# A seventh place for side work behind each gate and up group, and another layout of the second layer's staging tiles

## The chip, the cores and the metric

The kernel runs on one core of a Trainium2 chip. Its engines work side by side, each through its own queue, in order: TensorE (PE, with its weight loads shown as PEld), VectorE (DVE), ScalarE (ACT), GpSimd (POOL) and SyncE (SP), which here only issues DMAs. The metric is the device time of one execution in microseconds (us), the median of several. All arithmetic is in fp32; a product is made of three matmuls on operands that are split into a rounded part and the rest.

## The reference

2048 tokens of width 1024. What is computed, with the shapes:

```python
xn  = layernorm(x)                          # [2048, 1024]
q, k, v = split(xn @ wqkv)                  # 32 heads of 32
pq, pk  = phi(q), phi(k)                    # phi(t) = where(t > 0, t + 1, exp(t)) + 1e-6
kv, z   = pk.T @ v, sum(pk)                 # for each head, over all tokens
s   = ((pq @ kv) / (pq @ z + 1e-6)) @ wo    # [2048, 1024]
h   = silu(xn @ w1) * (xn @ w3)             # [2048, 3584]
g   = silu(h @ w2)                          # [2048, 1024]
out = x + s * g
```

Both branches start from the same normalised `xn`, so the kernel normalises once.

## The kernel before, in words

**Products.** Every large product is done as one level of a Strassen-Winograd scheme: seven products of blocks (named B11, T2, T3, T1, B21, T4, B22 after the right operand, with A11, S2, S3, S1, A12, A22, S4 on the left) stand for eight, and sums of blocks are formed before and after. `split` (L84) makes an operand: a cast on ACT (L90), then the rest by a subtraction on DVE (L91). `mm3` (L95) issues the three matmuls, L98 to L100, of 128x128 by 128x512 each.

**First layer.** The tokens are taken in two halves of 1024 (`half`, L524). For each half, `gemm` (L400) is run for 4 pairs of keys and values, then for 4 query groups, then for 14 pairs of a gate and an up group; each group is 84 matmuls. Between its products a group calls `catch_up` (L388), which takes one piece of side work: first a kv step of the keys and values that lie behind (`later`), then one step of a generator of jobs (`jobs`), up to its next `yield`. The instructions of that step are put behind given marks on their engines with `tc.issue_after`. A group has six such places. In half 0 the jobs are `next_work` (L666): preparing the other half's operands and the sums of blocks of w2 (stored to `wt_d`). In half 1 they are `attention_work` (L817): z, the denominators, the product of kv with wo (`merge_wo`, stored to `wp_d`) and `divide` (L740), which loads a block of phi(q) and of the reciprocals into a tile, multiplies on DVE (L757), forms four sums (L603 to L607) and stores to `qs_d` on POOL (L760). `go_on` (L697) loads two jobs ahead. What is left at the end of a half is issued in one go (`for j, _ in jobs: run(j)`).

The job tiles (`job_tile`, L120) are three buffers. The signed tiles (`signed`, L117) are four buffers that hold phi and silu results; the small tiles (`small`, L114) are six, under the tag `c`.

**Attention layer and second layer.** Both use `Segment` (L849): the right operand is kept split, and eight groups of 256 tokens run past it (`tokens`, L881). The attention layer multiplies the stored query blocks by the stored kv-wo blocks (`wp`); its operands for the first token group are loaded into job tiles (`queries`, L972), and its output goes to `s_d` from small tiles. Another 32 steps of divides run in its own places. Then the first layer's pools are closed and the late pools are laid over them, in the order of their creation. The second layer, h @ w2, runs as five segments over 4, 6, 6, 6 and 6 blocks of 128 rows of w2. The right operand's pieces are loaded one at a time into staging tiles (`second_weights`, L992, load at L994) and split into `pw`; in the last token group of a segment the next segment's pieces are loaded and split (`between`, L1034). Left operands are loaded by `hiddens` (L985, load at L989) into twelve tiles. In the last segment `finish` (L1011) loads a block of s (`ss`, L1014) and, for the last token group, of x (`xs`, L1017), applies silu on ACT (L1018), multiplies on DVE (L1019) and stores, for all but the last token group by an accumulating DMA onto an `out` that was filled with x before (`lay_x`, L1026).

**Order.** The program is unrolled. The framework orders each engine's instructions, and each DMA queue's, ahead of time by its own simulated clock; on the chip each queue then goes strictly in that order, and an instruction that waits holds what stands behind it. `tc.issue_after(x)` adds an edge on the queue of x alone: later instructions of that engine are issued behind x, without waiting for its end. A late tile waits for the earlier tiles that lay on its bytes.

Of the kernel before, what the change touches and what calls it, by code (L numbers as in the profile page):

```python
# [9 lines left out]
F32 = mybir.dt.float32  # L10
# [6 lines left out]
P = 128  # L17
C = 512
# [4 lines left out]
def tile_linear_attention_times_swiglu(  # L23
# [10 lines left out]
    nc = tc.nc  # L34
    x, out = x[0], out[0]
# [15 lines left out]
    def bank(name):  # L51
        return ps.tile([P, C], F32, tag="bank", name=name)
# [27 lines left out]
    s_d = [dram.tile([P, D], F32, name=f"s_d{t}") for t in range(S // P)]  # L80
# [33 lines left out]
    def small(name):  # L114
        return pc.tile([P, C], F32, tag="c", name=name)
# [263 lines left out]
    def product(acc, B, A, start, stop=True):  # L379
        K = ND // 2  # L380
        for k in range(K):
            mm3(acc, (B[:, 0, k], B[:, 1, k]), (A[:, 0, k], A[:, 1, k]),
                start=start and k == 0, stop=stop and k == K - 1)
# [4 lines left out]
    def catch_up(*marks):  # L388

        if later:  # L390
            later.pop(0)()
        elif jobs:
            job, in_order = jobs[0]
            with ExitStack() as behind:
                for m in marks + (tuple(fetched) if in_order else ()):
                    behind.enter_context(tc.issue_after(m.ins))
                if next(job, None) is None:
                    jobs.pop(0)

    def gemm(B, A, use, early=False, paired=False, own=False):  # L400

        name = B.name
        B.upto("B11")
        u = (st.tile([P, C], F32, tag="own", bufs=1, name=f"u{name}") if own else  # L410
             pe.tile([P, C], F32, tag="u", name=f"u{name}"))
        ba = bank(f"a{name}")
        product(ba, B.upto("B11"), A["A11"], True)
        copied = nc.scalar.copy(out=u, in_=ba)
        if early:
            catch_up(copied)
            yield
            product(ba, B.upto("B21"), A["A12"], False)
            use(0, 0, ba)
            yield  # L420
            for _ in B.stages:
                pass
        else:
            next(stages, None)
            catch_up(copied)
            if paired:
                yield
        bb, bc, bd = (bank(f"{n}{name}") for n in "bcd")
        product(bb, B.upto("T2"), A["S2"], True)
        added = nc.vector.tensor_add(out=u, in0=bb, in1=u)  # L430
        next(stages, None)
        catch_up(copied, added)
        if paired:
            yield
        product(bc, B.upto("T3"), A["S3"], True)
        c22 = small(f"c22{name}")
        added = nc.vector.tensor_add(out=c22, in0=bc, in1=u)
        next(stages, None)
        catch_up(copied, added)
        if paired:  # L440
            yield
        product(bd, B.upto("T1"), A["S1"], True)
        added = nc.vector.tensor_add(out=c22, in0=bd, in1=c22)
        use(1, 1, c22)
        next(stages, None)
        catch_up(copied, added)
        if paired:
            yield
        if not early:
            product(ba, B.upto("B21"), A["A12"], False)  # L450
            use(0, 0, ba)
            next(stages, None)
            catch_up(copied, added)
        if paired:
            yield
        product(bc, B.upto("T4"), A["A22"], False)
        c21 = small(f"c21{name}")
        added = nc.vector.tensor_add(out=c21, in0=bc, in1=u)
        use(0, 1, c21)
        next(stages, None)  # L460
        catch_up(copied, added)
        if paired:
            yield
        product(bd, B.upto("B22"), A["S4"], False)
        c12 = small(f"c12{name}")
        nc.vector.tensor_add(out=c12, in0=bd, in1=u)
        use(1, 0, c12)
        next(stages, None)

    def phi(src, dst, z=None):  # L470

        nc.scalar.activation(dst, src, AF.Relu, scale=-1.0)
        nc.scalar.activation(dst, dst, AF.Exp, scale=-1.0)
        nc.vector.scalar_tensor_tensor(dst, src, 0.0, dst, op0=ALU.max, op1=ALU.add, accum_out=z)  # L474
# [49 lines left out]
    def half(h):  # L524
        A = operand_tiles(h)

        def keys(pair, **how):
            return gemm(ops[f"k{h}_{pair}_"], A, uses[pair][0], **how)

        def values(pair, **how):  # L530
            return gemm(ops[f"v{h}_{pair}_"], A, uses[pair][1], **how)
# [44 lines left out]
        for pair in range(ND // 2):  # L576

            def use_q(n, c, src):
                j = 2 * pair + n
                pq = signed(f"pq{h}_{j}_{c}")  # L580
                phi(src, pq)
                nc.gpsimd.dma_start(out=pq_d[j // JG][2 * h + c][:, j % JG], in_=pq)  # L582

            run(gemm(ops[f"q{h}_{pair}_"], A, use_q))
# [385 lines left out]
    loads = []  # L970
# [21 lines left out]
    def second_weights(i, n, k):  # L992
        t = late_small(f"r{n}B{i}_{k}")
        nc.sync.dma_start(out=t, in_=second_weight(i, n, k))  # L994
        return t
# [13 lines left out]
    ADDED = NG - 1  # L1009

    def finish(m, t, n, a):  # L1011
        r0, cols = (2 * m + t) * P, slice(n * C, (n + 1) * C)
        ss = late_small(f"ss{m}_{t}{n}")
        nc.sync.dma_start(out=ss, in_=s_d[2 * m + t][:, cols])  # L1014
        if m >= ADDED:
            xs = late_small(f"xs{m}_{t}{n}")
            nc.sync.dma_start(out=xs, in_=x[r0:r0 + P, cols])  # L1017
        nc.scalar.activation(a, a, AF.Silu)  # L1018
        nc.vector.tensor_mul(a, a, ss)  # L1019
        if m >= ADDED:  # L1020
            nc.vector.tensor_add(a, a, xs)
            nc.gpsimd.dma_start(out=out[r0:r0 + P, cols], in_=a)
        else:
            nc.gpsimd.dma_start(out=out[r0:r0 + P, cols], in_=a, accum_op=ALU.add)
# [56 lines left out]
    def late_pool(name, bufs=1):  # L1081
        return ctx.enter_context(tc.tile_pool(name=name, bufs=bufs, reuse_waits="tile"))

    pu, pacc, pl, pw, pacc2, pd, px = (late_pool(*how) for how in (
        ("pu", 3), ("pacc",), ("pl", 6), ("pw",), ("pacc2",), ("pd", 2), ("px", 12)))

    def late_small(name):
        pool, tag = (pd, "d") if name.startswith("xs") else (pl, "c")
        return pool.tile([P, C], F32, tag=tag, name=name)

    def layer_place(n, i, k):
        return pw.tile([P, 2, C], FR, tag=f"{n}_{k}", name=f"{n}_{k}")
# [36 lines left out]
```

## Time and profile before

| | us |
|---|---|
| median of 3 runs | 2441.73 (2438.21 to 2448.21) |
| profiled execution, its own time | 2448.69 |
| span of its profile, first to last instruction | 2446.7 |
| TensorE busy in the span | 2337.9 |
| VectorE busy in the span | 1748.3 |
| ScalarE busy in the span | 939.0 |
| GpSimd busy in the span | 304.2 |
| mean granted TensorE clock | 0.983 |

The page gives each engine's busy time, the span in 40 slices of 61 us with the busy share in tenths, and the chain of work that ended last. By the order of time, the second half's groups begin at about 833 us; the attention layer's matmuls run from 1708.0 to 1862.8 us and the second layer's from 1873.2 to 2437.5 us. Rows of a timeline give the start, the duration (for merged instructions, from the first to the last), the engine, the line, the operation, out<-in, the count, and in brackets how long the engine had been idle and what ended that. SPq and POOLq are the queues that issue DMAs; the time there is that of issuing. A tile's number is left out of its name.

### The profile page before, as it was taken

The page shows a single profiled execution, that of the slowest core. Times are in us where ns is not written, and L with a number is a line of the kernel's source. Part 1 is how long each engine was busy: PE and PEld are TensorE (multiplying, and loading weights), DVE is VectorE, ACT ScalarE, POOL GpSimd, SP SyncE. Part 2 cuts the span into 40 slices and gives each one's busy share as a digit, 9 for nine tenths or more (in the row PEclk, how much of TensorE's full clock was granted, in tenths as well). Part 3 has the DMA queues.
Part 4 walks back from the last instruction along what each step waited for, and adds up shares of the span by engine and source line. Part 5 has one row for each costly group of instructions (what it writes and reads, how often), then busy time and mean ns, then how long its engine had stood idle before and what let it go on. Part 6 is the DMA issues. An engine that isn't in the chain of part 4 may idle for free.

```text
span 2446.7 us, 30779 instructions
## 1 busy us (share of the span) xinstructions
PE 2337.9 (96%) x10544; PEld 1935.9 (79%) x10544; DVE 1748.3 (71%) x3181; ACT 939.0 (38%) x1659; POOL 304.2 (12%) x397
## 2 busy tenths in 40 slices
PE   6999999999999999999999999992998999999987
PEld 5888888888888788888888888882886888878866
DVE  8755878787887665578777887785555577676776
ACT  4434644433323243455333333332323534242432
POOL 3000112121121200001111111111110000000032
PEclk9999999999999999999999999996998999999998
DMA  3211445475665831134454555347665566774696
GB/s 121 86 52 69 154 165 173 158 237 193 226 224 184 298 106 53 39 135 143 142 180 141 194 184 196 130 151 276 224 211 181 179 198 195 242 240 153 211 229 160
DMA packets 311932, 418.05 MB, mean 171 GB/s; under 512 B 20528, under 2 KB 242736, under 8 KB 311664
## 3 DMA queue, kind: packets, MB, share of 16 engines
q1 hardware_dynamic: 280800, 320.40, 40.8%
q0 software_dynamic: 30976, 95.71, 11.3%
q8 instruction: 82, 1.34, 0.2%
q14 instruction: 74, 0.61, 0.1%
HBM read 277.35 MB, written 146.01 MB: 173 GB/s over the span
## 4 chain that ended last, share of the span: by engine, by line
PE 84%; DMA 6%; issue 4%; DVE 3%; POOL 2%; SPq 1%; ACT 0%; POOLq 0%; ACTq 0%; DVEq 0%
PE cB L98 1%; PE cB L99 1%; PE cB L100 1%; PE dB L98 1%; PE dB L100 1%; PE dB L99 1%; PE aB L98 1%; PE aB L100 1%; PE aB L99 1%; PE kv L513 1%; DMA XA11B<-ho_d 1%; PE bB L98 1%; DMA qd<-pq_d 1%; PE bB L99 1%; PE bB L100 1%
## 5 line engine op out<-in xcount | busy, mean ns | idle before, releaser
L625 POOL DMA_DIRECT2D ho_d<-sg x56 | 51.2, 915 | 552.3 <-DVE sg L620 452.1
L582 POOL DMA_DIRECT2D pq_d<-pq x32 | 17.6, 550 | 484.1 <-DVE pq L474 481.0
L911 POOL DMA_DIRECT2D u_d<-uB x32 | 17.3, 542 | 417.6 <-DVE uB L894 367.5
L633 POOL DMA_DIRECT2D ho_d<-hs x60 | 54.6, 909 | 41.3 <-DVE hs L604 29.2
L623 POOL DMA_DIRECT2D ho_d<-sg x56 | 37.8, 674 | 102.5 <-DVE sg L620 96.1
L894 DVE TENSOR_TENSOR acc<-dB,acc 128x512 f32<-128x512 f32 x56 | 38.4, 686 | 13.6 <-PE dB L100 13.5
L98 PE MATMUL cB<-T,XA22B 128*128 128x512 f32 x87 | 36.1, 415 | 11.7 <-DVE acc L894 11.7
L90 ACT CAST XA11B<-XA11B 128x384 fp32r<-128x384 f32 (+1 forms) x40 | 19.7, 493 | 69.1 <-DMA XA11B<-ho_d 67.0
L760 POOL DMA_DIRECT2D qs_d<-qd x32 | 27.7, 869 | 134.1 <-DVE qd L607 64.5
L98 PE MATMUL B11s<-wp,XA11q 128*128 128x512 f32 x8 | 4.2, 530 | 39.9 <-ACT XA11q L90 39.9
L91 DVE TENSOR_TENSOR XS3B<-XS3B 128x384 fp32r<-128x384 f32 (+1 forms) x40 | 22.2, 556 | 25.8 <-ACT XS3B L90 25.5
L90 ACT CAST XS1B<-XS1B 128x384 fp32r<-128x384 f32 (+1 forms) x40 | 19.7, 493 | 52.1 <-DMA XS1B<-ho_d 45.8
L91 DVE TENSOR_TENSOR XA11B<-XA11B 128x384 fp32r<-128x384 f32 (+1 forms) x40 | 21.2, 529 | 25.5 <-ACT XA11B L90 25.5
L91 DVE TENSOR_TENSOR XS1B<-XS1B 128x384 fp32r<-128x384 f32 (+1 forms) x40 | 21.1, 529 | 25.0 <-ACT XS1B L90 24.9
L98 PE MATMUL dB<-B,XS4B 128*128 128x512 f32 x87 | 34.6, 398 | 3.1 <-DVE acc L894 3.1
L90 ACT CAST XS2B<-XS2B 128x384 fp32r<-128x384 f32 (+1 forms) x40 | 19.7, 493 | 45.2 <-DMA XS2B<-ho_d 42.5
L894 DVE TENSOR_TENSOR acc<-cB,acc 128x512 f32<-128x512 f32 x50 | 34.2, 684 | 3.7 <-PE cB L100 3.7
L91 DVE TENSOR_TENSOR XS2B<-XS2B 128x384 fp32r<-128x384 f32 (+1 forms) x40 | 21.3, 533 | 20.9 <-ACT XS2B L90 20.8
L513 PEld LDWEIGHTS kv<-kvr 128*128 128x128 f32 x256 | 33.5, 191 | 2.5
L757 DVE SCALAR_TENSOR_TENSOR qd<-qd 128x512 f32<-128x512 f32 x32 | 21.9, 683 | 18.8 <-DMA qd<-pq_d 18.8
L99 PE MATMUL cB<-T,XA22B 128*128 128x512 f32 x87 | 35.3, 405 | 0.0
L98 PE MATMUL aB<-B,XA12B 128*128 128x512 f32 x87 | 33.9, 390 | 1.4 <-ACT acc L1018 1.4
(5843 smaller groups left out, 8493.6 us busy)
## 6 DMA issues: line engine op xcount, KB each, us to landing
qs_d<-qd POOLq DMA_DIRECT2D x32, 512.0 KB, 4.3
ho_d<-hs POOLq DMA_DIRECT2D x60, 256.0 KB, 4.8
ho_d<-sg POOLq DMA_DIRECT2D x56, 256.0 KB, 4.0
w<-in_B_w SPq DMA_DIRECT2D x56, 256.0 KB
wt_d<-w SPq DMA_DIRECT2D x28, 512.0 KB
ho_d<-hs SPq DMA_DIRECT2D x52, 256.0 KB
pq_d<-pq POOLq DMA_DIRECT2D x32, 256.0 KB, 2.7
a_dS<-xo SPq DMA_DIRECT2D x16, 512.0 KB
```

The costliest lines, as they stand in the source:

```text
L90: nc.scalar.copy(out=hi, in_=src)
L91: return nc.vector.tensor_sub(out=lo, in0=src, in1=hi.bitcast(F32))
L98: nc.tensor.matmul(acc, lhsT=wh, rhs=ah, start=start, stop=False, skip_group_check=True)
L99: nc.tensor.matmul(acc, lhsT=wh, rhs=al, start=False, stop=False, skip_group_check=True)
L100: nc.tensor.matmul(acc, lhsT=wl, rhs=ah, start=False, stop=stop, skip_group_check=True)
L513: nc.tensor.matmul(acc, lhsT=r[:, 1, t], rhs=r[:, 0, t], start=t == 0, stop=t == C // P - 1)
L623: nc.gpsimd.dma_start(out=ho_d[i][2 * h + c][:, :, 0, k], in_=halves[:, :, 0])
L625: nc.gpsimd.dma_start(out=ho_d[i][2 * h + c][:, :, 1:3, k], in_=halves)
L633: queue.dma_start(out=ho_d[i][2 * h + c][:, :, 3 + 2 * e:5 + 2 * e, k], in_=o[e].rearrange("p (g n s) -> p g n s", n=2, s=P))
L757: nc.vector.scalar_tensor_tensor(t[:, :2], t[:, :2], 1e-6, t[:, 2:], op0=ALU.add, op1=ALU.mult)
L760: nc.gpsimd.dma_start(out=qs_d[m][:, :, k], in_=t.rearrange("p a (n s) -> p (a n) s", s=P))
L894: return V.tensor_add(out=c, in0=src, in1=c)
```

## The change

A group whose name begins with g or u (gate and up groups, not keys, values or queries) calls `catch_up` once more, behind its last product and its last sum, with the sum `c12` as a mark. The loads of `ss` and `xs` in `finish` are placed behind the last operand load that was traced before them (`loads[-1]`). The late pools are created in another order, with other sizes: `pl` (second weights, and three of the four `ss` of a token group) has four tiles instead of six; a new pool `pm` of two holds the `ss` of the place (1, 0); `pd` (`xs`) moves from behind `pacc2` to in front of `pl`. The first-layer tiles under `pl` were two small tiles and the four signed tiles before; after it they are the four signed tiles alone, and `pd` lies on those two small tiles.

```diff
@@ gemm @@
         product(bd, B.upto("B22"), A["S4"], False)
         c12 = small(f"c12{name}")
-        nc.vector.tensor_add(out=c12, in0=bd, in1=u)
+        added = nc.vector.tensor_add(out=c12, in0=bd, in1=u)
         use(1, 0, c12)
         next(stages, None)
+        if name[0] in "gu":
+            catch_up(copied, added)
@@ finish @@
-        ss = late_small(f"ss{m}_{t}{n}")
-        nc.sync.dma_start(out=ss, in_=s_d[2 * m + t][:, cols])
-        if m >= ADDED:
-            xs = late_small(f"xs{m}_{t}{n}")
-            nc.sync.dma_start(out=xs, in_=x[r0:r0 + P, cols])
+        ss = late_small(f"ss{m}_{t}{n}", pm if (t, n) == (1, 0) else None)
+        with tc.issue_after(loads[-1].ins):
+            nc.sync.dma_start(out=ss, in_=s_d[2 * m + t][:, cols])
+            if m >= ADDED:
+                xs = late_small(f"xs{m}_{t}{n}", pd)
+                nc.sync.dma_start(out=xs, in_=x[r0:r0 + P, cols])
@@ pools @@
-    pu, pacc, pl, pw, pacc2, pd, px = (late_pool(*how) for how in (
-        ("pu", 3), ("pacc",), ("pl", 6), ("pw",), ("pacc2",), ("pd", 2), ("px", 12)))
-
-    def late_small(name):
-        pool, tag = (pd, "d") if name.startswith("xs") else (pl, "c")
-        return pool.tile([P, C], F32, tag=tag, name=name)
+    pu, pacc, pd, pl, pw, pacc2, pm, px = (late_pool(*how) for how in (
+        ("pu", 3), ("pacc",), ("pd", 2), ("pl", 4), ("pw",), ("pacc2",), ("pm", 2), ("px", 12)))
+
+    def late_small(name, pool=None):
+        return (pool or pl).tile([P, C], F32, tag="c", name=name)
```

## The prediction

> **What bounds the kernel now.** I read the slices and the chain of waits of the page first, then the list of who waited for whom, then the order of time where TensorE stands still.
>
> ```profile
> PE   6999999999999999999999999992998999999987
> PE 84%; DMA 6%; issue 4%; DVE 3%; POOL 2%; SPq 1%; ACT 0%; POOLq 0%; ACTq 0%; DVEq 0%
> ...
> PE B11s L98 <- ACT XA11q L90: 39.9, 1, 39.9
> PE cB L98 <- DVE acc L894: 11.7, 5, 3.8
> PE B11B L98 <- ACT B L90: 11.6, 2, 10.2
> PE dB L98 <- DVE acc L894: 3.1, 2, 2.7
> PE aB L98 <- ACT acc L1018: 1.4, 1, 1.4
> ```
>
> TensorE (PE) carries 84% of the chain, so a change pays only where PE idles. The slices name three places besides the start: the 28th (a 2, about 1651 to 1713 us), the 31st (an 8) and the end. The waits (total, times, longest) give their causes: 39.9 us for the first operand of the attention layer, 10.2 us for the first weight of the second layer, and, in its last segment, 16.2 us in pieces (11.7 + 3.1 + 1.4).
>
> **First part: the seventh place.** PE around the end of the second half of tokens:
>
> ```profile
> 1654.71 0.39 PE L100 MATMUL du__13518<-S,T1u__13367 128*128 128x512 f32 x1
> 1659.72 0.77 PE L98 MATMUL cu__13517<-A,T4u__13452 128*128 128x512 f32 x1 [4.62 <-DVE c22u__13544 L437]
> ...
> 1667.69 0.39 PE L100 MATMUL du__13518<-S,B22u__13471 128*128 128x512 f32 x1
> 1708.00 0.80 PE L98 MATMUL B11s<-wp,XA11q 128*128 128x512 f32 x1 [39.93 <-ACT XA11q L90]
> ...
> 1713.21 0.40 PE L98 MATMUL T2s<-wp,XS2q 128*128 128x512 f32 x1
> ```
> ```profile
> 1704.24 0.80 SPq L982 DMA_DIRECT2D r0q<-qs_d  x2
> 1707.33 0.62 ACT L90 CAST XA11q<-r0q 128x512 fp32r<-128x512 f32 x1 [18.54 <-DMA r0q<-qs_d]
> L661 SPq DMA_DIRECT2D wt_d<-w x28: 519/562/1896, 518.1 to 776.5; - x28
> ```
>
> The operand XA11q is loaded at 1704.24, behind the last divide jobs, whose staging tiles (three of them) it shares. Why are divides running there? Count the steps (yields). Half 0: 4 prepare_next of 21 and 28 weight_sums of 3, 168. Half 1: 1 (spread_z) + 48 (denominators) + 60 (merge_wo) + 96 (24 divides of 4), 205. Places: 32 groups (q, gate, up) of 6 are 192, of which 5 go to the last keys and values. So half 0 fits and ends 19 places early; half 1 lacks 18 places, and these 18 steps, four and a half divides, run as a tail. The wt_d row confirms the counting: 32 groups of 19.1 us (84 matmuls) end with the half near 833 us, so place 173 of 192, the last one used, falls at 773; the last store starts at 776.5. With a seventh place in 28 groups there are 220 places, 215 for side work: the 205 steps end ten places, some 27 us, before the half does.
>
> What goes: from 1654.94 (end of the last fast matmul) to 1708.00 PE does 24 matmuls, 5.4 us at the 0.227 us each of the row below; 47.6 us are lost. The first 12 matmuls after it take 5.21 instead of 2.72 us (half clock after idling), 2.5 more: 50.1 us at most. What is late next: the 4.62 us wait and its slow matmuls (12 at 0.43 from 1659.72 to 1664.98, 2.5 us) come from weight tiles wp whose casts wait for their loads, and those loads stay. That leaves 43. The DMAs are the other limit (columns of a stretch: its length, the busy time of PE, PEld, DVE, ACT and POOL with counts, granted clock, DMA share, GB/s).
>
> ```profile
> 1651.00:1668.00 17.00, 12.38 (x43) 9.39 (x41) 11.79 (x22) 6.34 (x12) 0.91 (x1) 0.80 1.04 367
> 1651.00:1708.00 57.00, 12.45 (x43) 9.39 (x41) 31.48 (x72) 13.79 (x25) 11.15 (x13) 0.63 0.78 276
> 1651.00:1708.00 57.00, 9.75 (x30) 5.13 (x6) 0.63 0.78 276
> 1130.00:1640.00 510.00, 509.03 (x2243) 420.45 (x2242) 399.79 (x716) 183.06 (x314) 72.21 (x99) 1.00 0.50 165
> qs_d<-qd POOLq DMA_DIRECT2D x32, 512.0 KB, 4.3
> qd<-r_d SPq DMA_DIRECT2D x64, 128.0 KB
> qd<-pq_d SPq DMA_DIRECT2D x64, 128.0 KB
> r0q<-qs_d SPq DMA_DIRECT2D x30, 256.0 KB
> ACT wp L90 <- DMA wp<-wp_d: 25.0, 4, 9.7
> ```
>
> The 57 us move 15.7 MB (276 GB/s). The third row is the divides' alone (DVE and POOL): six of them, 512 KB in (four loads) and 512 KB out, 6.3 MB that go; seven operands of 256 KB, 1.8 MB, come into this stretch. 11.2 MB at 367 to 276 GB/s take 31 to 41 us, to 1682 to 1692; the last weight piece must still be split and multiplied, some 5 us. In before, the first token tile ends at 1708 + 19.1 + 2.5 = 1729.6, so the gain is 33 to 43. DVE is no limit: 31.48 less 9.75 us. I take 40; bounds 20 (below) and 43.
>
> The moved steps keep their DMAs, now on SP and POOL during the gate and up groups: there DVE is idle 110 of 510 us, 4.1 per 19.1 us group, and the loads of a divide are asked for seven places ahead, 22 us before and 19 after, against landings of 4.3 us median for its store. On SP they stand ahead of the raw weight loads, which run at least a group ahead, and of the hs stores, on POOL between the ho_d stores; a late one reaches PE only through those. In half 0 the same work only ends earlier. PE lost 1 of 510 us there. I cost it at nothing; if that cover went, a seventh of a 1 us wait in each of 56 groups would be 8 us.
>
> **Second part: the tiles.**
>
> ```profile
> 1863.02 0.81 SPq L1017 DMA_DIRECT2D xs<-in_A_x  x2
> 1869.69 0.33 SPq L994 DMA_DIRECT2D rB11B<-in_B_w  x1
> 1873.19 0.79 PE L98 MATMUL B11B<-B,XA11B 128*128 128x512 f32 x1 [10.21 <-ACT B L90]
> ...
> 1880.39 0.40 PE L98 MATMUL T4B<-T,XA22B 128*128 128x512 f32 x1
> SPq L1017 <- PE B22s L100: 13.5, 1, 13.5
> SPq L994 <- DMA s_d<-s: 5.7, 1, 5.7
> ```
>
> The first weight load stands on SP behind an xs load that waits 13.5 us for the last attention matmul, then waits 5.7 us more for a store of s, because its tile lies on an accumulator of that layer. The change orders xs behind the last operand loads and lays the four pl tiles exactly on the four signed tiles, free once the last up group is stored. Four of the seven first pieces can then be staged before the layer ends, and their places free up as its last tile proceeds. Lost in before: 10.4 us, and 13 matmuls in 7.2 instead of 2.95 us, 4.2: 14.6 together. I take 13; bounds 5 (another wait in the same queue) and 14.6.
>
> ```profile
> 2320.00:2430.00 110.00, 93.84 (x384) 74.14 (x384) 80.63 (x128) 34.09 (x65) 37.31 (x38) 0.95 0.85 203
> 2340.00:2350.00 10.00, 4.88 (x20) 3.78 (x21) 6.73 (x13) 2.72 (x6) 2.23 (x4) 1.00 1.04 240
> 2344.56 5.35 SPq L1014 DMA_DIRECT2D ss<-s_d  x2
> 2350.01 0.37 SPq L989 DMA_DIRECT2D XS3B<-ho_d  x1
> SPq L1014 <- DVE acc L1019: 64.3, 24, 7.5
> ```
>
> In the last segment the ss loads wait on SP for tiles that the product with ss (L1019) frees, 64.3 us in all, and operand loads stand behind them: XS3B leaves at 2350.01, DVE waits for it in order, PE for DVE. Behind XS4B of the next tile, two sevenths into the current one, every ss tile is already free, and what queues behind ss on SP, the operands of the tile after next, is needed a tile (14 us) later. PE could gain its 16.2 us and what the clock of 0.95 costs in 93.84 us, 4.7: 21. But the DMA engines are busy 0.85 of these 110 us, 94 us: at a full share at most 16 go. I take half, 8; below nothing, an ss that lands late holds DVE's queue: -4. The Trainium skill, page "DMA: Bandwidth & Descriptors", section "Specifications", limits a core's HBM traffic to about 358 GB/s; by it the 22 MB of this stretch need an estimated 62 us, nothing binds, and the term is 21. The trace disagrees so far: a share of 1.04 at 240 GB/s.
>
> Weights have four staging tiles instead of six at each of four changes of segment.
>
> ```profile
> 2289.61 0.33 SPq L994 DMA_DIRECT2D rB11B<-in_B_w  x1
> ...
> 2293.74 0.33 SPq L994 DMA_DIRECT2D rB22B<-in_B_w  x1
> 2295.18 0.33 SPq L994 DMA_DIRECT2D rB11B<-in_B_w  x1
> ...
> 2313.01 0.68 DVE L91 TENSOR_TENSOR B<-rB22B,B 128x512 fp32r<-128x512 f32 x1
> 2313.70 0.39 PE L98 MATMUL B22B<-B,XS4B 128*128 128x512 f32 x1
> ```
>
> A tile comes round after 4.13 us (six pieces on, 2289.61 to 2293.74); pieces leave every 0.80 us (seven in 5.57). Four tiles give one per 1.03 us: 17 pieces behind the first four lose 17 x 0.23 = 4 us. There is no slack: PE uses the last piece as its split ends (2313.70). Evictions in DVE's queue may hide part, so -2.5 at each, -10; bounds 0 and -16.
>
> Sum: 40 + 13 + 8 - 10 = 51 us. The profiled execution took 2448.69 us (span 2446.7), 7 above the median; the same 51 from the median 2441.73 give 2391.
>
> **Rivals.** (1) Four staging tiles hurt in full (-16) and the reordered loads lose 2: 40 + 13 - 2 - 16 = 35, 2407; for it speaks that PE has no slack there, against it that DVE has other work to do. 0.16. (2) The attention layer's start finds another wait: the wp casts wait 25.0 us for loads in before, and ScalarE takes them in order. The first term is 20, the time 2411. 0.11. (3) The last segment is not DMA bound and the staging costs nothing: 40 + 13 + 21, 2368; the page's rule would have it so, the shares of 1.04 speak against it. 0.08. (4) Slower: steps now stand in DVE's queue between c12 and the next group's first sums, and PE waits in each of 56 groups. It turns the sign at 51/56 = 0.9 us a group; at 1.5 us (84 us) the time is 2475. DVE's 4.1 idle us a group speak against it. 0.05. (5) It doesn't do what it says, and the tail of divides stays because something else holds them: 13 + 8 - 10 = 11, 2431. The wt_d row makes the counting sound. 0.05.
>
> **Numbers.** The forecast keeps 0.55. A measurement can tell about 0.5%, 12 us. Faster by more: 0.55 + 0.16 + 0.11 + 0.08 less 0.02 for the tail of (2), 0.88; within: (5) and that tail, 0.07; slower: (4), 0.05. The range 2368 to 2418 takes in (1), (2), (3) and leaves out (4), (5) and the far ends of D and A, the staging and the first term, together under 0.2.
>
> **What would show it.** The wt_d stores end near 708 us (24 places in the q groups, then 149 at seven a group); no divide stands between the last up group and the attention layer, and PE's wait before B11s is under 10 us; B11B follows B22s without 10 us of idling; L1014 waits for L1019 only a little. Wrong would be: B11s still late (first term), new PE waits for B or T splits at the segment changes (staging), or PE waits under L430 and L437 within the groups (rival 4).

## The result, and the profile after

The changed kernel takes 2400.46 us (median of 4 runs, 2396.22 to 2404.65) where the kernel before takes 2440.82 (4 runs, 2438.21 to 2448.21): a ratio of 0.983, interval 0.9802 to 0.9857. That is 40.4 us less, where 51 were forecast. The profiled executions are further apart: 2448.69 (span 2446.7) against 2400.58 (span 2398.5), 48.2 us of span, because the one of before took longer than any of its four timed runs, 7.9 above their median, and the one of after lies at its median. The parts below are compared on the spans.

From the page of the changed kernel, the PE slices and the chain of waits; under them the list of what PE waited for (total, times, longest):

```profile
PE   6999999999999999999999999999998999999997
PE 86%; DMA 7%; DVE 3%; issue 1%; ACT 1%; POOL 1%; SPq 0%; POOLq 0%; DVEq 0%; ACTq 0%
...
PE T1s L98 <- ACT wp L90: 4.6, 1, 4.6
PE cB L98 <- DVE acc L896: 4.1, 4, 2.7
PE B11B L99 <- DVE B L91: 4.1, 1, 4.1
PE B11B L98 <- ACT B L90: 4.0, 3, 1.8
PE aB L98 <- DVE uB L896: 2.5, 2, 1.6
```

The slice with a 2 is gone, and with it the wait of 39.9 us for the attention's first operand and the 10.2 us in front of the second layer. "issue" falls from 4% to 1% of the chain. Behind the kernel's start (where PE waits 11.3 us before its first transposes, 12.1 in before) what is left on PE are waits under 5 us, and four of these five rows are new or at new places: a wp cast inside the attention (T1s), the split of the second layer's first piece (B11B L99), casts of staged weights at the changes of segment (B11B L98), and a sum of the last segment (aB).

To see where the 48.2 us come from, take the start of each matmul in the order of time of PE, and call lost what lies between two starts beyond the 0.2268 us of undisturbed ones:

| stretch | before | after | gain |
|---|---|---|---|
| last attention matmul starts at | 1862.60 | 1818.74 | 43.9 |
| from there to the layer's first matmul, and lost in its first 126 | 10.6 + 6.0 | 0.2 + 11.1 | 5.3 |
| lost in the last 84 and the first 84 matmuls around each of the four changes of segment | 3.7 | 14.6 | -10.9 |
| lost in the last segment behind its first 84 | 23.9 | 11.6 | 12.3 |
| start of the last matmul to the end of the span | 9.4 | 11.4 | -2.0 |

The sum is 48.6. The starts are read to 0.01 us and only what lies above 0.2268 is counted. That alone adds about 0.002 us a matmul: up to 1.4 us where 672 matmuls are counted, 0.7 in the last segment and 0.2 in the first 126. It is nearly alike in every kernel, so differences between kernels stand; the 0.4 us by which this sum is over comes from it.

The steps of half 0, first row (the stores of the sums of w2, first and last start before the "; -"), and SP's wait for the ss tiles; then three stretches of the changed kernel (columns as in the prediction), the first with the start of the attention, the second with that of layer two, the third the last segment:

```profile
L663 SPq DMA_DIRECT2D wt_d<-w x28: 519/562/563, 496.9 to 713.5; - x28
SPq L1017 <- DVE acc L1022: 16.8, 8, 3.9
...
1655.00:1720.00 65.00, 60.37 (x260) 49.12 (x259) 46.82 (x84) 25.10 (x45) 14.00 (x20) 0.97 0.80 272
1820.00:1850.00 30.00, 24.45 (x89) 17.87 (x89) 22.28 (x40) 14.98 (x30) 2.71 (x5) 0.89 0.75 249
2281.00:2391.00 110.00, 99.16 (x422) 79.37 (x421) 89.01 (x143) 38.97 (x74) 39.69 (x41) 0.98 0.91 230
```

The last of these stores starts at 713.5 us where before's started at 776.5, with 708 forecast: the seventh place carries side work earlier, as counted. The wait on SP for ss tiles falls from 64.3 to 16.8 us, and in 110 us of the last segment PE starts 422 matmuls where it started 384. Layer two now begins without a gap but stumbles at its second product. SP, ACT, DVE and PE there, in the order of time on each queue:

```profile
1801.32 0.37 SPq L996 DMA_DIRECT2D rB11B<-in_B_w  x1
...
1815.08 0.59 ACT L922 COPY us<-B11s 128x512 f32<-128x512 f32 x1 [8.84 <-PE B11s L100]
1815.57 0.62 ACT L90 CAST B<-rB11B 128x512 fp32r<-128x512 f32 x1
...
1817.86 0.69 DVE L923 TENSOR_TENSOR s<-B21s,us 128x512 f32<-128x512 f32 x1 [11.13 <-ACT T L90]
...
1822.31 0.68 DVE L896 TENSOR_TENSOR s<-B22s,s 128x512 f32<-128x512 f32 x1
1822.91 0.68 DVE L91 TENSOR_TENSOR B<-rB11B,B 128x512 fp32r<-128x512 f32 x1
...
1818.96 0.39 PE L98 MATMUL B11B<-B,XA11B 128*128 128x512 f32 x1
1819.19 0.39 PE L98 MATMUL T2B<-T,XS2B 128*128 128x512 f32 x1
1823.64 0.79 PE L99 MATMUL B11B<-B,XA11B 128*128 128x512 f32 x1 [4.06 <-DVE B L91]
1824.23 0.63 PE L100 MATMUL B11B<-B,XA11B 128*128 128x512 f32 x1
1823.61 0.33 SPq L996 DMA_DIRECT2D rB21B<-in_B_w  x1
```

The piece's load is issued at 1801.32, 17 us early, but its cast stands on ACT behind a copy that waits for the attention's last group, and its split on DVE behind that group's sums. Both engines had stood idle before these (8.84 and 11.13 us), so by these rows it is the order of their queues that holds the piece, and not a lack of their time. PE can use the cast part at once and then waits 4.06 us for the rest, at a lower clock for some 4 us more. The fifth piece's load (rB21B) is issued only when this split has freed a tile, at 1823.61.

### The profile page after: what moved, and what is told of

It is laid out like the page before. It is cut to its first block, busy times and chain, and to the rows that moved or that the text cites. A ratio compares the mean times of both kernels' runs of the same rounds, so it can differ in the third digit from the quotient of the medians.

```text
span 2398.5 us, 30756 instructions
## 1 busy us (share of the span) xinstructions
PE 2337.2 (97%) x10544; PEld 1932.0 (81%) x10544; DVE 1745.6 (73%) x3181; ACT 935.9 (39%) x1659; POOL 304.3 (13%) x397
## 3 DMA queue, kind: packets, MB, share of 16 engines
q0 software_dynamic: 30976, 95.71, 11.4%
## 4 chain that ended last, share of the span: by engine, by line
PE 86%; DMA 7%; DVE 3%; issue 1%; ACT 1%; POOL 1%; SPq 0%; POOLq 0%; DVEq 0%; ACTq 0%
PE cB L98 1%; PE dB L100 1%; PE cB L100 1%; PE dB L99 1%; PE dB L98 1%; PE cB L99 1%; PE aB L100 1%; PE aB L98 1%; PE aB L99 1%; PE kv L515 1%; DMA wp<-wp_d 1%; PE bB L100 1%; PE bB L99 1%; PE bB L98 1%; PE den L727 1%
## 5 line engine op out<-in xcount | busy, mean ns | idle before, releaser
L98 PE MATMUL cB<-T,XA22B 128*128 128x512 f32 x87 | 35.2, 405 | 5.7 <-DVE acc L896 4.1
L98 PE MATMUL aB<-B,XA12B 128*128 128x512 f32 x87 | 34.0, 391 | 2.5 <-DVE uB L896 2.5
L91 DVE TENSOR_TENSOR XA12B<-XA12B 128x384 fp32r<-128x384 f32 (+1 forms) x40 | 23.9, 596 | 15.7 <-ACT XA12B L90 15.7
L90 ACT CAST XS1B<-XS1B 128x384 fp32r<-128x384 f32 (+1 forms) x40 | 19.6, 491 | 39.9 <-DMA XS1B<-ho_d 29.0
L91 DVE TENSOR_TENSOR XS3B<-XS3B 128x384 fp32r<-128x384 f32 (+1 forms) x40 | 21.7, 541 | 18.4 <-ACT XS3B L90 17.8
L91 DVE TENSOR_TENSOR XS2B<-XS2B 128x384 fp32r<-128x384 f32 (+1 forms) x40 | 21.1, 528 | 19.0 <-ACT XS2B L90 18.7
L98 PE MATMUL dB<-B,XS4B 128*128 128x512 f32 x87 | 34.0, 390 | 0.7 <-DVE acc L896 0.7
L92 ACT ACTIVATE pqs<-pqd 128x512 fp32r<-128x512 f32 x32 | 20.2, 631 | 36.7 <-PE den L727 5.5
L99 PE MATMUL cB<-T,XA22B 128*128 128x512 f32 x87 | 34.4, 395 | 0.0
L100 PE MATMUL cB<-T,XA22B 128*128 128x512 f32 x87 | 34.4, 395 | 0.0
```

The costliest lines, as they stand in the source:

```text
L90: nc.scalar.copy(out=hi, in_=src)
L91: return nc.vector.tensor_sub(out=lo, in0=src, in1=hi.bitcast(F32))
L98: nc.tensor.matmul(acc, lhsT=wh, rhs=ah, start=start, stop=False, skip_group_check=True)
L99: nc.tensor.matmul(acc, lhsT=wh, rhs=al, start=False, stop=False, skip_group_check=True)
L100: nc.tensor.matmul(acc, lhsT=wl, rhs=ah, start=False, stop=stop, skip_group_check=True)
```

## The experiments

One table holds all kernels; each time is a median beside the median of the kernel before on the same chip, and the columns behind are read from the matmul starts as above (attention: lost from its first matmul to its last; start of layer two: gap + lost in its first 126). In the kernels that reach the attention early, 24 matmuls of the last up group, 5.4 us of work, run among its 672; they are not lost time and are not in the column, but the 13 us of the expectation of e7_late, and the 4 to 6 of its theory, have them in. Chips differ by some us, so rows of different chips are compared by their ratios.

| kernel | us | before | ratio (interval) | attention | start of layer two | four changes | last segment |
|---|---|---|---|---|---|---|---|
| before | 2440.82 | | | 3.9 | 10.6 + 6.0 | 3.7 | 23.9 |
| after | 2400.46 | 2440.82 | 0.983 (0.9802 to 0.9857) | 8.0 | 0.2 + 11.1 | 14.6 | 11.6 |
| e1_places | 2406.38 | 2442.98 | 0.9845 (0.9827 to 0.9863) | 7.8 | 10.4 + 8.0 | 2.6 | 20.3 |
| e2_tiles | 2438.60 | 2442.98 | 0.9984 (0.9972 to 0.9997) | 3.6 | 0.2 + 8.8 | 13.5 | 13.4 |
| e4_order | 2434.62 | 2442.98 | 0.9965 (0.9953 to 0.9977) | 3.6 | 10.4 + 5.5 | 3.3 | 12.4 |
| e6_twowaits | 2396.93 | 2442.98 | 0.9809 (0.9791 to 0.9827) | 10.8 | 6.7 + 4.8 | 1.6 | 22.1 |
| e3_six | 2399.57 | 2444.24 | 0.9809 (0.9791 to 0.9828) | 7.4 | 15.4 + 3.8 | 3.6 | 13.3 |
| e5_layout | 2412.59 | 2444.24 | 0.9869 (0.9851 to 0.9887) | 9.6 | 7.7 + 10.1 | 12.5 | 18.7 |
| e7_late | 2392.98 | 2444.24 | 0.9782 (0.9764 to 0.9799) | 1.5 | 0.2 + 10.1 | 12.5 | 11.0 |
| e8_both | 2394.48 | 2444.24 | 0.9791 (0.9774 to 0.9809) | 1.8 | 15.3 + 4.8 | 2.4 | 13.8 |
| e9_inorder | 2390.25 | 2446.14 | 0.9766 (0.9749 to 0.9783) | 1.5 | 0.2 + 8.7 | 2.8 | 15.2 |
| e10_small | 2381.37 | 2446.14 | 0.9736 (0.9721 to 0.9750) | 2.0 | 6.2 + 6.8 | 2.0 | 12.3 |
| e11_pool | 2393.76 | 2446.14 | 0.9786 (0.9770 to 0.9803) | 1.5 | 0.2 + 11.6 | 14.7 | 12.4 |
| e12_plain | 2375.61 | 2442.37 | 0.9727 (0.9711 to 0.9743) | 3.3 | 6.2 + 5.8 | 2.3 | 6.1 |

**The change taken apart: places, tiles.** e1_places is the kernel before with the one edit in `gemm`; e2_tiles is the changed kernel without it.

```diff
@@ gemm, to before (e2_tiles: the reverse, to after) @@
-        nc.vector.tensor_add(out=c12, in0=bd, in1=u)
+        added = nc.vector.tensor_add(out=c12, in0=bd, in1=u)
         use(1, 0, c12)
         next(stages, None)
+        if name[0] in "gu":
+            catch_up(copied, added)
```

> The kernel before with the seventh place alone. Theory (the parts add up; the places give the attention's earlier start): the last attention matmul comes some 44 us earlier, the segments of the second layer cost what they cost before (changes 3.7 us, last segment 24 us of lost matmul time), and the gap in front of layer two stays at about 16 us: about 2397 us beside 2441 (ratio 0.982). Rival (the places gain only together with the new layout, because an attention that ends earlier finds its staging tiles still taken): the gap in front of layer two grows by 10 us or more, 2407 us or above.

> The changed kernel without the seventh place: layout and ordered loads alone. Theory (parts add up): -5 us at the layer's start, -12 in the last segment, +11 at the four segment changes, +2 behind the last matmul: -4 us, 2437 beside 2441, within what can be told from no change. Rival (the layout is what lets the attention end earlier): 2415 us or below, with the last attention matmul more than 20 us earlier than before.

e1_places gains 36.6 us, 7 less than its theory; e2_tiles gains 4.4, as its theory had it. Together they make 41.0, and the change makes 40.4: the parts add up. In e1_places the last attention matmul starts at 1816.64, 46 us earlier than before, and the second layer is nearly as it was: the gap of 10.4 us stands, its first matmuls lose 2 us more, the four changes lose 2.6, the last segment 20.3. The rival, that an earlier attention would make the gap grow, falls. The span of its profile, 2402.9, is 43.8 us under before's, as the theory had it; but the theory was taken from before's profiled execution, which lies 5.7 us above the median of 2442.98, and that is most of the 7 us that the medians lack.

**Is it the place or the count?** The prediction counted 205 steps against 187 places. e6_twowaits leaves six places and takes one empty step out of each divide: 24 in half 1, which makes 181, and 8 in the divides of the attention layer's own places.

```diff
@@ divide, to before @@
-            for _ in range(3):
+            for _ in range(2):
                 yield True
```

> The kernel before with six places, but the divide's three empty steps cut to two, so that its steps fall from 205 to 181 and fit the places there are. Theory (the number of places against the number of steps decides, not where the seventh place stands): no divide stands between the last up group and the attention, and the time falls by about 40 us, to some 2400 (0.983). Rival 1 (the seventh place gains because its work stands behind the last sum of a group): less than 15 us. Rival 2 (the empty steps hide a wait, and without them engines stand still in the groups): the attention starts earlier, but the groups grow by as much, 2435 or above.

46.0 us, more than the seventh place gives by itself. Two rows of e6_twowaits, the groups of half 1 and the stores of half 0:

```profile
1130.00:1640.00 510.00, 510.00 (x2248) 421.65 (x2247) 413.21 (x762) 185.69 (x318) 78.10 (x107) 1.00 0.55 179
L661 SPq DMA_DIRECT2D wt_d<-w x28: 518/562/1739, 518.9 to 777.2; - x28
```

In half 0 nothing has moved (777.2 against 776.5). In the same 510 us of half 1 DVE does 413 us of work where before had 399.8, since divides of the old tail now run there, and PE doesn't wait once: 2248 matmuls at 0.227 us fill the stretch. So the count of steps against places is what held the attention, and no place behind the last sum is needed for it.

**Order against layout.** e4_order puts only the `tc.issue_after` around ss and xs into the kernel before; e5_layout takes only that out of the changed kernel.

```diff
@@ finish, to before (e5_layout: dropped from after) @@
+        with tc.issue_after(loads[-1].ins):
             nc.sync.dma_start(out=ss, in_=s_d[2 * m + t][:, cols])
             ...
```

> The kernel before with its ss and xs loads issued behind the last load of its segment, in the old layout. Theory (the order of the loads is what the last segment gains by; the six staging tiles are what the segment changes had): the last segment loses some 12 us of matmul time in place of 24 and the changes stay at 4: 2429 us beside 2441 (ratio 0.995). Rival (the last segment gains by the new places of ss and xs, not by the order): the last segment loses 20 us or more and the time stays within 4 us of before.

> The changed kernel without the order of the ss and xs loads: places and layout alone. Theory (the order is what the last segment gains by): the last segment loses some 24 us of matmul time as before the change, 2412 us (0.988). Rival (with tiles of their own the loads are early enough in any order): the last segment loses 12 us as in the changed kernel, 2400.

In the last segment the order alone brings the loss from 23.9 to 12.4, about all that the change brings there; the layout without the order leaves 18.7, which the theory had at 24: the layout, which gives one ss of four a pool of its own, helps a little, and on top of the order it adds nothing that can be seen (11.6). In time e4_order gains 8.4 of the 12 expected. e5_layout lands where it was expected, but by two misses that cancel: its last segment loses 5 us less, and its gap in front of layer two is 7.5 us longer than in the changed kernel. Closing that gap needs both edits. What SP did at the end of the attention in e4_order, and then in e5_layout:

```profile
SPq L994 <- DMA s_d<-s: 19.9, 1, 19.9
1866.34 0.34 SPq L994 DMA_DIRECT2D rB11B<-in_B_w  x1
```

```profile
SPq L1017 <- PE B22s L100: 17.8, 1, 17.8
1816.01 0.80 SPq L1017 DMA_DIRECT2D ss<-s_d  x2
1816.89 0.46 SPq L996 DMA_DIRECT2D rB11B<-in_B_w  x1
```

With the order alone the first weight load leads SP's queue, and waits 19.9 us for a store of s whose tile lies under its own. With the layout alone its tile is free, but an ss load stands ahead of it and waits 17.8 us for the last attention product. Either wait alone keeps most of the gap (10.4 and 7.7); with both gone it is 0.2.

**Four tiles against six.** e3_six stages the second layer's pieces in all six tiles of `pl` and `pm` in turn (`staged` is a list of the pieces so far).

```diff
@@ second_weights, to after @@
-        t = late_small(f"r{n}B{i}_{k}")
+        staged.append(n)
+        t = late_small(f"r{n}B{i}_{k}", pm if len(staged) % 6 in (5, 0) else None)
```

> The changed kernel, its second layer's weights staged in all six tiles of the two pools in turn (four and two), ss and xs where they are. Theory (four tiles in place of six are what the segment changes lost by): the matmul time lost at the four changes falls from 15 us to about 4, the wait in front of layer two from 11 to about 8: 2387 us beside the changed kernel's 2400 (0.978 of before). Rival (the changes lose by the order of ACT's and DVE's queues, whatever the number of tiles): the changes still lose 12 us or more, 2398 to 2402.

The four changes lose 3.6 instead of 14.6: the tiles were their cause, and the rival falls. But the time is not 2387. Of the 11 us gained, 7.9 are lost again at the start of layer two (19.2 in place of 11.3) and 1.7 in the last segment. SP and PE at the start of layer two:

```profile
SPq L999 <- PE B22s L100: 17.9, 1, 17.9
1818.46 0.33 SPq L999 DMA_DIRECT2D rB21B<-in_B_w  x1
...
1828.60 0.38 SPq L999 DMA_DIRECT2D rB11B<-in_B_w  x1
PE B11B L98 <- ACT B L90: 15.0, 1, 15.0
```

The framework's ordering ahead of time put rB21B, the fifth piece, whose tile lies in `pm`, at the head of SP's queue. On the chip that tile comes free with the attention's last product, and rB11B, which PE needs first, leaves 27 us later than in the changed kernel (1828.60 against 1801.32).

e9_inorder keeps the six tiles and fixes the order of the loads by an edge from each piece to the next; it also holds the edit of e7_late, below.

```diff
@@ second_weights, to e7_late @@
-        t = late_small(f"r{n}B{i}_{k}")
-        nc.sync.dma_start(out=t, in_=second_weight(i, n, k))
+        pool = pm if len(staged) % 6 in (4, 5) else None
+        t = late_small(f"r{n}B{i}_{k}", pool)
+        with tc.issue_after(staged[-1].ins) if staged else ExitStack():
+            staged.append(nc.sync.dma_start(out=t, in_=second_weight(i, n, k)))
```

> The changed kernel with the late work's loads behind the last wp load, six staging tiles in turn, and every weight load of the second layer issued behind the one before it. Theory (six tiles cure the segment changes; the kernel of eight lost it in front of layer two because a load into a tile still in use stood ahead of the others in SP's queue): the changes lose about 4 us as in the six-tile kernels, the gap in front of layer two stays at 0.2 us as with four tiles, the time is 2382 us beside 2393 with late loads alone (0.975 of before). Rival (the two tiles that lie elsewhere come free too late in any order): gap and first products lose 15 us or more, 2390 or above.

The changes lose 2.8, the gap is 0.2 again: the cause of e3_six is shown. The time, 55.9 us under before, stands between theory and rival. Its last segment loses 15.2 where e7_late loses 11.0, and that is not explained. Its last attention matmul also starts 5.0 us later than e7_late's (1818.42 against 1813.40), though PE's instructions are the same up to there. The wait of this row, in a group of half 0, stands in e9_inorder's profile and makes most of it (its clock falls for a while, too); e7_late has 0.6 us there with the same instructions, so a single profile can be some us off without an edit:

```profile
PE dg__4298 L98 <- DVE c22g__4334 L443: 3.3, 1, 3.3
```

**The attention's new wait.** Inside the attention the changed kernel loses 8.0 us where before lost 3.9. SP's issues there, in the changed kernel:

```profile
1658.13 0.57 SPq L751 DMA_DIRECT2D qd<-r_d  x1
1658.84 1.37 SPq L1065 DMA_DIRECT2D wp<-wp_d  x2
1660.71 0.94 SPq L753 DMA_DIRECT2D qd<-pq_d  x1
...
1670.22 2.72 SPq L1065 DMA_DIRECT2D wp<-wp_d  x2
1683.11 0.79 PE L98 MATMUL T1s<-wp,XS1q 128*128 128x512 f32 x1 [4.63 <-ACT wp L90]
```

Loads of `late_work` (the last 32 steps of divides, for token groups that the attention reaches much later) stand between the last wp loads, which now hold PE. e7_late keeps each wp load as a mark (`fetched`) and puts the late work behind the last one.

```diff
@@ program, to after @@
-    jobs.append((late_work(), False))
+    jobs.append((late_work(), True))
@@ attention_right @@
-                nc.sync.dma_start(out=place[:, o, 1].bitcast(F32) if raw is None else raw[:, o], in_=wp_d[g][:, o])
+                fetched[:] = [nc.sync.dma_start(out=place[:, o, 1].bitcast(F32) if raw is None else raw[:, o], in_=wp_d[g][:, o])]
```

> The changed kernel, the loads of the late work (the queries that the attention does not need yet) issued behind the last wp load. Theory (PE's wait of 4.6 us and the lower clock behind it inside the attention come from wp loads that queue behind these): the attention loses 4 to 6 us in place of 13, 2393 us (0.980). Rival (the wait is for the transfers' bandwidth, whatever the order): the loss stays, 2400, or moves to the late work's own reader, 2400 to 2410.

The same stretch of e7_late, and its wp loads:

```profile
1655.00:1720.00 65.00, 65.00 (x288) 53.83 (x287) 50.83 (x94) 26.81 (x47) 15.50 (x23) 1.00 0.84 296
1659.29 5.58 SPq L1065 DMA_DIRECT2D wp<-wp_d  x6
```

The six loads leave together by 1665, PE fills the stretch (65.00 of 65.00, 288 matmuls in place of 260, clock 1.00 in place of 0.97), and the time falls to 2392.98 where 2393 was expected (51.3 us under before on its chip, where the changed kernel is 40.4 under). The attention loses 1.5 us, no more than the reading of the starts adds; counted as in the expectation, with the up group's 24 matmuls, it is 6.9, a little over the theory's 4 to 6. The DMA engines carried more (296 against 272 GB/s), so it was the order and not their limit. e8_both adds e3_six's tiles to this:

> The changed kernel with both: six staging tiles in turn, and the late work's loads behind the last wp load. Theory (they touch different stretches and add up): 2380 us (0.975). Rival (the time that the attention gains is lost again in front of layer two): no faster than the better of the two alone.

It is no faster than e7_late, but not for the reason of its rival: the gap of 15.3 us is that of e3_six (15.4), with its SP order.

**The start of layer two.** e11_pool makes the low parts of the layer's first four pieces on POOL, so that they don't stand behind the attention's sums on DVE (`by` is the engine of the subtraction).

```diff
@@ Segment.right, to e7_late @@
-                split(self.Y[n, k], raw)
+                split(self.Y[n, k], raw, by=nc.gpsimd if self.name == "B0" and k == 0 and i < 4 else None)
```

> The changed kernel with the late work's loads behind the last wp load, and the low parts of the second layer's first four weight pieces made on POOL in place of DVE. Theory (the first products of layer two wait because these splits stand behind the attention's last seven sums in DVE's queue, and the fifth piece's load waits for the tile that the split frees): PE's wait of 4 us at the second product group goes, the fifth load is issued 5 us earlier, the first 126 matmuls lose 4 to 6 us in place of 10, 2388 us beside 2393. Rival (the casts on ACT or the transfers end as late): they lose 9 us or more, 2392 to 2395.

Nothing is gained: the first 126 matmuls lose 11.6. POOL and PE there:

```profile
1815.14 1.14 POOL L1008 DMA_DIRECT2D s_d<-s  x2 [0.66 <-DVE s L896]
1816.29 1.27 POOL L91 TENSOR_TENSOR B<-rB11B,B 128x512 fp32r<-128x512 f32 x1
PE B11B L99 <- POOL B L91: 5.6, 1, 5.6
```

The split now stands behind the stores of s on POOL, and these wait for the same last sums on DVE; a piece takes 1.27 us there (0.69 on DVE, by its rows). The fifth load isn't early either: rB21B leaves 6.4 us behind the start of the last attention matmul (1817.59 against 1811.19), in the changed kernel 4.9 (1823.61 against 1818.74). The wait has moved from one queue to another. So it is shown that PE waits for the split and that the split's engine is held by the attention's last sums; a version with the splits ahead of these was not tried.

**The small version.** e10_small leaves before's layout and six places, and makes three edits: two empty steps (e6_twowaits), the order of ss and xs (e4_order), the order of the late work's loads (e7_late).

> The kernel before with six places, the old layout and three small edits: two empty steps in the divide in place of three, ss and xs loads behind the last load of their segment, the late work's loads behind the last wp load. Theory (the three touch different stretches and add up): 2397 with the empty steps alone, less 10 in the last segment, less 8 in the attention: 2379 us (0.974). Rival (an earlier attention loses again what the order gains): 2390 or above.

2381.37 us, a ratio of 0.9736 (0.9721 to 0.9750): faster than the changed kernel (0.9802 to 0.9857), with less of it. Each of the three shows in its own stretch: no divides before the attention, 2.0 lost in it (10.8 with the empty steps alone), 12.3 in the last segment; and with six tiles the changes lose 2.0.

**What the last segment still loses.** e12_plain is e10_small with plain stores of `out` (the addition of x is left out for seven of eight token groups).

```diff
-            nc.gpsimd.dma_start(out=out[r0:r0 + P, cols], in_=a, accum_op=ALU.add)
+            nc.gpsimd.dma_start(out=out[r0:r0 + P, cols], in_=a)
```

> The kernel of the three small edits, with out stored plainly in place of being added to the x laid there; this leaves out the addition of x for seven of eight token tiles. The adding stores take 34% of the 16 DMA engines for 8.4 MB where the other transfers take 40% for 18.3 MB. Theory (what the last segment still loses, 12 us, is waits for operands that land late because the DMA engines are full): the last segment loses 2 to 6 us, 2372 to 2377 beside 2381. Rival (the loss comes from the order of the loads on SP or of the sums on DVE, and the DMA engines have time left): it loses 10 us or more, and the time stays within 3 us of 2381.

The same 100 us of the last segment, e10_small and then e12_plain: the stretch, and the queue that holds the stores (packets, MB, share of the 16 engines):

```profile
2265.00:2365.00 100.00, 92.13 (x392) 73.71 (x391) 79.20 (x130) 34.27 (x66) 38.53 (x38) 0.98 0.95 235
q0 software_dynamic: 3963, 7.23, 44.4%
PE cB L98 <- DVE acc L894: 7.2, 5, 2.2
```

```profile
2265.00:2365.00 100.00, 92.22 (x400) 74.17 (x398) 85.46 (x138) 34.31 (x65) 28.20 (x39) 0.99 0.71 238
q0 software_dynamic: 2400, 7.87, 19.4%
PE cB L98 <- DVE acc L894: 3.7, 4, 1.3
```

The rate that the trace counts is the same (235 and 238 GB/s), the share falls from 0.95 to 0.71, and the loss of the last segment from 12.3 to 6.1 us, at the edge of the theory's 2 to 6. The time does not settle it: the medians lie 5.8 us apart but come from two chips, and beside before on the same chip the two kernels are 64.8 and 66.8 us faster, with intervals that overlap. So it is by the profile that half of what is left there comes from the adding stores, and what fell with them is the time of the DMA engines, not the rate.

## Why the prediction was right, point by point

The result lies 9 us above the forecast of 2391, inside its range. That the sum came so near is in part luck: the second term came out 7.7 us short and the third 4.3 over.

**The first term** (40) was right in mechanism and in size: 43.9 against before's profile, 39 to 41 against two others with the same instructions up to there (below). The count of 205 steps against 187 places is what e6_twowaits confirms from the other side. The prediction kept "the last weight piece must still be split and multiplied" and 31 to 41 us of DMA time as limits; the wp loads did become the next wait, as rival (2) said, but for 4.6 us in place of 20, and e7_late shows that this was their order on SP.

**The second term** is the one that was mis-sized: 13 forecast, 5.3 measured. The gap went as argued (10.6 to 0.2), and e4_order and e5_layout show that it needed both the order and the layout. What failed is the step "four of the seven first pieces can then be staged before the layer ends, and their places free up as its last tile proceeds". They were loaded before it ended, but a tile comes free with its split, which stood on DVE behind the last tile's sums: the first 126 matmuls lose 11.1 in place of 6.0.

**The third term** was taken at 8, half of the 16 us that the DMA engines' share seemed to leave; it measured 12.3. The share does limit PE there, but half was a guess: in e12_plain the share falls and the segment loses 6 us less. Rival (3), by which nothing binds there, would have given 21 and is refuted with it. The Trainium skill, page "DMA: Bandwidth & Descriptors", section "Specifications", by which rival (3) was priced, gives a limit in bytes per second, about 358 GB/s. That limit is not the bound here: at 235 and 238 GB/s, both well below it, e10_small loses 12.3 us in its last segment and e12_plain 6.1.

**The fourth term** (-10) measured -10.9, and e3_six and e9_inorder give it back with six tiles. Every kernel with four staging tiles loses 12.5 to 14.7 us there, every one with six 1.6 to 3.7, so the number of tiles was the right cause; the 1.03 us a piece from which the size was worked out was not read again.

**The cost taken at nothing** was nearly nothing. In half 1 PE is busy 508.9 of 510 us in e1_places and 509.0 before. In half 0's groups each of the eight kernels with the seventh place has one wait of PE for a sum on DVE (L437 or L443), 0.2 to 3.3 us long, and none of the six with six places has one: the mechanism of rival (4) exists, in one group and not in 56. In e9_inorder, where that wait is longest, it makes most of 5 us.

**Not in the sum** were 2.0 us behind the last matmul, and that the profiled execution of before took longer than others of its kernel. The parts measure 48 us between profiles, near the forecast's 51, but 40 between medians: the prediction worked its sum out of an execution 7 us above the median and then took it whole from the median. Part of these 7 us can be placed. e2_tiles and e4_order issue the same instructions as before up to the end of the attention, and start its last matmul at 1858.06 and 1859.27, 4.5 and 3.3 us sooner than before's 1862.60. One piece is the wait of this row, near the start of half 1, which is 1.0 us in e4_order and missing in e2_tiles:

```profile
PE ak__7058 L98 <- DMA A<-a_dA: 2.9, 1, 2.9
```

Most of the rest lies in the first 125 us, where the two reach their 500th matmul 2.1 and 1.5 us sooner. Against these two profiles the first term is 39.3 and 40.5 us in place of 43.9. What else made the execution longer stays open, since there is no second profile of before.

## What to carry to other kernels

Where side work runs in fixed places, count its steps against the places first: an empty step in each job can cost a whole tail, and taking it out was worth more here (46.0 us) than adding a place (36.6). A load that is issued early is early only if nothing on its queue waits ahead of it, its tile is free, and the engines that make it usable are not held by the work that it is to overlap; check all three in the trace of before. When a buffer changes its pool, look at the order of the queue again, because an order planned ahead by a simulated clock may put a load that waits long in front, as in e3_six.

## What was not expected of the hardware

Adding stores hold the DMA engines about 2.5 times as long per byte as plain ones from the same queue: 44.4% of 100 us for 7.23 MB against 19.4% for 7.87 MB, 6.1 against 2.5 us per MB. The adding stores also go in smaller packets (3963 of 1.8 KB on average against 2400 of 3.3 KB); how much of the difference is that and how much the adding, no run shows.

The seven other kernels with the seventh place, and the changed one, end 11.2 to 11.9 us behind the start of their last matmul; those with six places 9.1 to 9.8 (10.6 with plain stores). But for the kind of store in e12_plain the work there is the same in all, and the cause is open.
